# Moving columns of the matmuls read from both halves in turn

## The chip, the cores and the metric

One core of a Trainium2 chip runs the whole program. Its engines work side by side: TensorE (matmuls; PE in the profile, its weight loads PEld), VectorE (DVE), ScalarE (ACT), GpSimd (POOL) and the sync engine (SP), which here only issues transfers. TensorE writes to psum, eight banks of 512 fp32 columns on 128 partitions; DVE and ACT read it. The metric is the device time of one execution in microseconds; a kernel is told by the median of its runs.

In a matmul one operand, the weights, stands in the array, and the other, the moving one, is read column by column. A psum column comes out for each moving column.

## What is computed

```python
# x: 1 x 2048 x 576;  32 heads of 18;  F = 4608
xn = layernorm(x)                                   # no scale, no bias
q, k, v = split(xn @ wqkv)                          # per head
s = (softmax(q @ k.T * 18 ** -0.5) @ v) @ wo        # full attention
g = silu((relu(xn @ W_gate) * (xn @ W_up)) @ W_down)
return x + s * g
```

All is fp32. To keep fp32's accuracy with the faster F32R operands, the kernel splits a matrix into a high and a low part and adds three products (high·high, high·low, low·high); the probabilities and v use plain fp32 operands.

## The kernel before

**Two lanes.** Most matmuls use 64 of the 128 rows of the array, so that two of them, one on rows 0 to 63 and one on rows 64 to 127, run at once. The class `Lanes` writes out the order of the two lanes ahead of time, in Python, when the program is built. It keeps a clock for each lane, for the banks and for DVE ("V") and ACT ("A"). It counts a matmul as `cols * COL + FIX`, and each eviction by a length given in the code (0.685 for a row maximum, 0.6 for an exponential, 0.69 for the product of gate and up). It picks what each lane does next: `main` parts (sums over many matmuls) or `scores` (a matmul by itself), as banks come free. The chip then follows this order whatever the true times are; what must be waited for is waited for by semaphores.

**Stages.**
1. *Start.* Rows of x are loaded in groups of 512 tokens (`load_rows`: group 0 by four loads, groups 1 to 3 by one each). Meanwhile TensorE is warmed up (`busy`). Its 32 matmuls are 8 of ones, then groups of four: columns in order, and four forms of reading the same 512 columns (`mixed`): `b=2` (every second column first, then the others), `a=2` (0, 256, 1, 257, ...), `b=16` (steps of 16) and `a=32, c=4` (four neighbours, then a jump of 16). The last four read in order, with 32 weight columns instead of 128.
2. *Features, q, k, v.* For each group of 512 tokens, x is normalized, transposed by TensorE (`tps`) and stored as high and low parts with the tokens along the columns (`x`; spilled to `xTd`). Then come q and k (`pq`, the tokens of x moving, 512 columns; split on eviction by `split_full`, stored to `qd` and `kd`) and v (`pv`, 128 tokens of x as weights, 288 columns of `wv` moving; evicted by ACT L583, stored to `vd`).
3. *Feed-forward and attention together.* 144 units of the feed-forward net, each 128 features of F for 512 tokens: gate (`pg`) and up (`pu`), 27 matmuls of 512 columns on each, with the tokens of x moving. Two units make a cycle. `down` of an earlier pair of units runs in the same cycle: `py`, with 128 tokens of `hh` as weights and 288 columns of `dw` moving, 96 matmuls, added up in `ys`. Into this order are mixed the attention's scores: `pm` (scores of 128 queries against 512 keys, of which DVE takes the row maxima, L401) for the next pair of heads, and `psx` (128 keys against 512 queries, of which ACT takes the exponential, L891) for the present one. After a cycle, `attend` multiplies the probabilities with v in one burst (`po`, 64 records). There are eight cycles with only some maxima, then 64 with a burst each.
4. *End.* Attention output (`od`) times `wo` (`pw`, 128 rows, 288 columns moving) in groups of 128 tokens, times the gate (`gt`, from `yd` or `ys`; L1121), plus x (`xr`; L1122), stored by POOL's queue.

All matmuls but the transposes pass through `mm` (L274, L275), and so all have line 275 in the profile; the names of the tiles tell them apart. Loads pass through `load` (L271) on SP's queue, in the order of the code.

Of the kernel before, what the change touches and what calls it, by code (L numbers as in the profile page):

```python
# [9 lines left out]
F32 = mybir.dt.float32  # L10
F32R = mybir.dt.float32r
AF = mybir.ActivationFunctionType
ALU = mybir.AluOpType
# [15 lines left out]
class Lanes:  # L29


    COL, FIX, EVICT, SERVE, FENCE = 0.000446, 0.006, 0.28, 0.08, 0.15

    def __init__(self, banks, make, matmul, fence):
        self.make, self.matmul, self.fence = make, matmul, fence
# [182 lines left out]
def kernel(  # L218
# [10 lines left out]
    nc = tc.nc  # L229
    P = 128  # L230
# [13 lines left out]
    HC = D // 2  # L244
    HW = 2 * DH
# [10 lines left out]
    x2 = x.rearrange("b s d -> (b s) d")  # L256
    out2 = out.rearrange("b s d -> (b s) d")

    def rows512(t, g):
        return t[g * 512 : (g + 1) * 512, :].rearrange("(j p) d -> p j d", p=P)  # L260

    def pool(stack, name, bufs, side="left", **kw):
        return stack.enter_context(tc.tile_pool(name=name, bufs=bufs, side=side, reuse_waits="tile", **kw))
# [1 line left out]
    def keep(ins):  # L265
        return tc.keep_in_program_order(ins)
# [3 lines left out]
    def load(*args):  # L270
        ins = nc.sync.dma_start(*args)  # L271
        return keep(ins) if in_order[0] else ins

    def mm(*args, **kw):  # L274
        return keep(nc.tensor.matmul(*args, **kw))  # L275

    def tp(*args):
        return keep(nc.tensor.transpose(*args))
# [14 lines left out]
    def bank(b, name):  # L293
        return banks.tile([P, 512], F32, tag=f"b{b}", name=name)

    def fence(by, ps):
        eng = {"A": nc.scalar, "V": nc.vector}[by]
        eng.clobber_nop(outs=[eng.lower_ap(ps)])

    lanes = Lanes(8, bank, mm, fence)  # L300

    def lane_rows(lane):
        return slice(lane * R, (lane + 1) * R)

    def split_full(dhi, dlo):
        return [
            ("A", 0.6, lambda ps: nc.scalar.activation(dhi(), ps, AF.Copy)),
            ("V", 0.69, lambda ps: nc.vector.tensor_tensor(dlo(), ps, dhi().bitcast(F32), ALU.subtract)),
        ]

    def split_pool(hi, lo, raw):
# [5 lines left out]
    def pair(names, xt, ops, cols, steps):  # L317

        parts = []
        for o in range(2):  # L320
            def lane_ops(lane, o=o):
                places = [(4 * o + i, i) for i in range(KX - 1)]
                if lane == o:
                    places.append((KS - 1, KX - 1))
                rows = lane_rows(lane)
                return [
                    (lambda s=s, i=i, a=a, b=b: ops(rows, s, a, xt[o][i][rows, b, :]))
                    for s, i in places
                    for a, b in PRODUCTS
                ]  # L330

            parts.append(Part(names[o], o, [lane_ops(o), lane_ops(1 - o)], cols, steps[o]))
        return parts
# [97 lines left out]
    with ExitStack() as st:  # L431
# [19 lines left out]

        def load_rows(g):
            xt = one.tile([P, 4, D], F32, name="xt", bufs=2)
            if g == 0:
                for j in range(4):
                    load(xt[:, j], x2[j * P : (j + 1) * P, :])
            else:
                load(xt, rows512(x2, g))
            return xt

        def stats(xt, ln):
# [112 lines left out]
        def v_pairs(gw, g):  # L574
            pairs = []
            evs = {}

            def steps(j, m):
                def fn(ps):
                    if (j // 2, m) not in evs:  # L580
                        evs[j // 2, m] = [hp.tile([P, VN, 2, HW], F32, tag="hh", name="ev", bufs=4), 0]
                    ev = evs[j // 2, m]
                    nc.scalar.activation(  # L583
                        ev[0][:, :, j % 2, :], ps[:, :HC].rearrange("p (u d) -> p u d", d=HW), AF.Copy
                    )
                    ev[1] += 1
                    if ev[1] == 2:
                        t0 = g * 4 + j // 2 * 2
                        nc.gpsimd.dma_start(
                            vd[m * VN : (m + 1) * VN, :, t0 : t0 + 2, :].rearrange("u p t d -> p u (t d)"),  # L590
                            ev[0].rearrange("p u t d -> p u (t d)"),
                        )

                return [("A", 0.41, fn)]

            for j in range(4):
                js = slice(j * P, (j + 1) * P)
                pairs.append(
                    pair(
                        ("pv", "pv"), (xs[g], xs[g]),  # L600
                        lambda rows, s, a, xr, js=js: (xr[:, js], gw[rows, a, s, :]),
                        HC, [steps(j, m) for m in range(2)],
                    )
                )
            return pairs

        def busy(xt):

            ones = one.tile([P, 512], F32R, name="ones")
            xr = one.tile([P, 576], F32R, name="xr")  # L610
            root = one.tile([P, 1], F32, name="root")
            nc.gpsimd.memset(ones.bitcast(F32), 1.0)
            nc.scalar.activation(root, ident[:, :1], AF.Sqrt)
            nc.scalar.activation(xr, xt[:, 0], AF.Copy)
            ps = bank(7, "wu")
            def mixed(form, **n):
                return xr[:, :512].rearrange(f"p {form}", **n)

            ops = [(ones[:, :P], ones)] * 8 + [(xr[:, :P], xr[:, :512])] * 4
            ops += [(xr[:, :P], mixed("(a b) -> p b a", b=2))] * 4  # L620
            ops += [(xr[:, :P], mixed("(a b) -> p b a", a=2))] * 4
            ops += [(xr[:, :P], mixed("(a b) -> p b a", b=16))] * 4
            ops += [(xr[:, :P], mixed("(a b c) -> p b a c", a=32, c=4))] * 4
            ops += [(xr[:, :32], xr[:, :512])] * 4
            for l, r in ops:
                m = l.shape[1]
                to = ps[:m]
                if len(r.shape) == 3:
                    to = to.rearrange("p (a b) -> p a b", b=r.shape[2])
                if len(r.shape) == 4:  # L630
                    to = to.rearrange("p (a b c) -> p a b c", b=r.shape[2], c=r.shape[3])
                mm(to, l, r, start=True, stop=True)
            nc.scalar.activation(root, ps[:, :1], AF.Copy)

        ln0 = []
        xt0 = load_rows(0)
        busy(xt0)
        for _ in stats(xt0, ln0):
            pass
# [6 lines left out]

        qk_weights(0)
        nxt = load_rows(1)
        xn0 = one.tile([P, 4, D + DT], F32, name="xn")
        first_rows(*ln0, xn0)  # L650
# [317 lines left out]
    for k in range(0, N1, 2):  # L968
        i = k // 2
# [5 lines left out]
        n = 7 if i % 2 == 0 else 6  # L975
# [57 lines left out]
    def load_heads(k):  # L1033
        o = fo.tile([P, 5, P], F32, name="o")
        ks = slice(k * P, (k + 1) * P)
        nc.sync.dma_start(o[:, :4], od[:C4, ks].rearrange("(c p) t -> p c t", p=P))
        for d in range(2):
            nc.sync.dma_start(o[d * DT : (d + 1) * DT, 4], od[C4:, ks])
        return o

    def load_gate(k):
        if k // 4 == units[-1][0]:
            gt = ys[k % 4]
        else:
            gt = f2.tile([P, D], F32, name="gt")
            nc.sync.dma_start(gt, yd[k * P : (k + 1) * P, :])
        sg = f2.tile([P, D], F32, name="sg", bufs=2)
        nc.scalar.activation(sg, gt, AF.Sigmoid)
        nc.gpsimd.tensor_tensor(gt, gt, sg, ALU.mult)
        return gt  # L1050

    def load_res(k):
        xt = f2.tile([P, D], F32, name="xr")
        nc.sync.dma_start(xt, x2[k * P : (k + 1) * P, :])
        return xt
# [3 lines left out]
    def any_bank(name):  # L1059
        turns[0] += 1  # L1060
        return bank(turns[0] % 8, name)
# [27 lines left out]
    for j in range(4):  # L1089
        js = slice(j * P, (j + 1) * P)  # L1090
        for n in range(2):
            cs = halves[n]
            ps = any_bank("py")[:, :HC]
# [8 lines left out]
    for i, k in enumerate(horder):  # L1102
        if i + 3 < NT:
            ops_[i + 3] = load_heads(horder[i + 3])
        if i + 2 < NT:
            xts[i + 2] = load_res(horder[i + 2])
            gts[i + 2] = load_gate(horder[i + 2])
            hq[i + 2] = heads(ops_.pop(i + 2))
        hh, o5 = hq.pop(i)
        gt, xt = gts.pop(i), xts.pop(i)  # L1110
        for cs in halves:
            ps = any_bank("pw")[:, :HC]
            prs = []
            for c in range(4):
                ks = slice(c * P, (c + 1) * P)
                w = wos[c]
                prs += [(hh[:, 0, ks], w[:, 0, cs]), (hh[:, 0, ks], w[:, 1, cs]), (hh[:, 1, ks], w[:, 0, cs])]
            prs += [(o5, wos[4][:, a, cs]) for a in range(2)]
            for n, (l, w) in enumerate(prs):
                mm(ps, l, w, start=(n == 0), stop=(n == len(prs) - 1))  # L1120
            nc.vector.tensor_tensor(gt[:, cs], ps, gt[:, cs], ALU.mult)  # L1121
            nc.vector.tensor_tensor(xt[:, cs], xt[:, cs], gt[:, cs], ALU.add)  # L1122
        nc.gpsimd.dma_start(out2[k * P : (k + 1) * P, :], xt)
    acc.close()
    fin.close()
# [26 lines left out]
```

## Time and profile before

| | us |
|---|---|
| median of 3 runs | 2611.54 |
| lowest, highest | 2608.88, 2612.35 |
| profiled execution | 2609.53 |
| its span, first to last instruction | 2607.8 |
| around the span | 1.73 |

The mean granted clock of TensorE was 0.996 of full speed in the profiled execution. It read 192.79 MB from memory and wrote 44.96 MB.

How to read what follows: a group has its line, engine, operation, the tile written and those read, the shapes and the count; behind the bar its busy time, the mean ns of one, and the idle time of its engine just before it with what ended that. For matmuls, `64*128 64x512` means 64 rows and 128 weight columns, and 512 moving columns. A row of a timeline or of the chain begins with start and length in us. A matmul's record is longer than its share of the time, since the next begins before it has drained: the pace is the distance between starts.

### The profile page before, as it was taken

The numbers are of one execution on the slowest core, as the hardware profiler recorded it, in microseconds if no ns is written. First come the engines' busy times: TensorE is split into PE (matmuls) and PEld (weight loads), VectorE is DVE, ScalarE is ACT, GpSimd is POOL, SyncE is SP. The second block draws the span as 40 slices with busy tenths as digits, with TensorE's granted clock in tenths as the row PEclk, the third lists the DMA queues.
The fourth block names the chain that finished last, engine by engine and source line by source line (L and its number), as shares of the span: only waits on it lengthen the run. The fifth ranks groups of instructions, "written<-read, shape, count | busy, mean of one in ns | idle before, by whom it ended". The sixth has DMA issues, their size and how long they took to land.

```text
span 2607.8 us, 62736 instructions
## 1 busy us (share of the span) xinstructions
PE 2575.4 (99%) x25308; PEld 2106.7 (81%) x25308; DVE 1785.9 (68%) x2976; ACT 1471.0 (56%) x2763; POOL 1440.5 (55%) x1276
## 2 busy tenths in 40 slices
PE   8999999999999999999999999999999999999998
PEld 6998887777778887777778778788878777777778
DVE  4326557777777777777777777777777777776137
ACT  3221136666666666666666666666666666666662
POOL 4236885555555555555555555555555555555554
PEclk8999999999999999999999999999999999999999
DMA  7645332222332222222242222222232222222237
GB/s 240 219 150 150 88 103 69 78 70 72 98 100 66 76 69 75 69 70 75 74 133 72 71 72 67 74 66 77 72 114 82 66 77 72 74 67 58 58 113 214
DMA packets 270353, 241.85 MB, mean 93 GB/s; under 512 B 33904, under 2 KB 214896, under 8 KB 270064
## 3 DMA queue, kind: packets, MB, share of 16 engines
q1 hardware_dynamic: 262000, 209.53, 27.5%
q0 software_dynamic: 8064, 28.32, 3.3%
q8 instruction: 200, 3.28, 0.5%
q14 instruction: 89, 0.73, 0.1%
HBM read 192.79 MB, written 44.96 MB: 91 GB/s over the span
## 4 chain that ended last, share of the span: by engine, by line
PE 92%; DMA 3%; POOL 2%; DVE 1%; SPq 1%; issue 1%; ACT 0%; POOLq 0%; DVEq 0%; ACTq 0%
PE pg L275 19%; PE po L275 17%; PE py L275 16%; PE pu L275 15%; PE pm L275 10%; PE psx L275 9%; PE pq L275 3%; PE pv L275 2%; SPq L271 1%; PE pw L275 1%; DMA rgw<-in_A_wqkv_dram 0%; DMA qd<-hh 0%; DMA gt<-yd 0%; DMA rg<-in_B_W_up_dram 0%; DMA kT<-kd 0%
## 5 line engine op out<-in xcount | busy, mean ns | idle before, releaser
L401 DVE TENSOR_REDUCE mx<-pm 128x1 f32<-128x512 f32 x2048 | 1378.5, 689 | 351.5 <-PE pm L275 207.1
L891 ACT ACTIVATE p<-psx 128x512 f32<-128x512 f32 x2048 | 1181.9, 598 | 567.4 <-PE pm L275 279.3
L275 PE MATMUL pg<-x,gw 64*128 64x512 f32 x3888 | 1155.2, 391 | 1.8 <-POOL gw L313 1.8
L275 PE MATMUL pu<-x,gw 64*128 64x512 f32 x3888 | 1141.7, 391 | 0.0
L275 PE MATMUL pm<-kT,qT 54*128 54x512 f32 x2048 | 792.2, 397 | 0.7 <-DMA kT<-kd 0.7
L275 PE MATMUL psx<-qT,kT 56*128 56x512 f32 x2048 | 786.7, 394 | 0.0
L275 PEld LDWEIGHTS pg<-x,gw 64*128 64x128 f32 x3888 | 718.5, 186 | 43.4 <-POOL gw L313 2.7
L275 PEld LDWEIGHTS pu<-x,gw 64*128 64x128 f32 x3888 | 716.2, 186 | 33.5
L275 PE MATMUL py<-dw,hh 64*128 64x288 f32 x6864 | 720.3, 295 | 5.7 <-DVE ot L929 3.1
L275 PEld LDWEIGHTS py<-dw,hh 64*128 64x128 f32 x6864 | 665.4, 186 | 74.2 <-issue 53.4
L275 PE MATMUL po<-p,va 128*32 128x512 f32 x4096 | 452.7, 594 | 0.4 <-ACT p L891 0.4
L744 POOL CAST hh<-h 128x512 fp32r<-128x512 f32 x127 | 77.6, 611 | 607.2 <-DVE h L741 607.2
L313 POOL TENSOR_TENSOR gw<-rg,gw 128x1152 fp32r<-128x1152 f32 x144 | 383.7, 2665 | 11.6
L275 PEld LDWEIGHTS psx<-qT,kT 56*128 56x128 f32 x2048 | 375.3, 185 | 17.8
L275 PEld LDWEIGHTS pm<-kT,qT 54*128 54x128 f32 x2048 | 371.6, 185 | 15.6 <-DVE mx L401 0.9
L771 POOL TENSOR_TENSOR y<-yt,y 128x288 f32<-128x288 f32 x268 | 215.0, 806 | 297.8 <-ACT yt L770 297.6
L275 PEld LDWEIGHTS po<-p,va 128*32 128x32 f32 x4096 | 126.4, 110 | 279.1 <-issue 269.1
L313 POOL TENSOR_TENSOR dw<-rd,dw 128x576 fp32r<-128x576 f32 x144 | 212.2, 1474 | 11.5
L747 POOL TENSOR_TENSOR hh<-h,hh 128x512 fp32r<-128x512 f32 x144 | 186.2, 1293 | 33.2 <-ACT hh L746 23.1
L312 POOL CAST gw<-rg 128x1152 fp32r<-128x1152 f32 x144 | 165.0, 1146 | 23.4 <-DMA rg<-in_B_W_up_dram 9.5
L766 DVE TENSOR_TENSOR y<-py,y 128x288 f32<-128x288 f32 x268 | 120.0, 448 | 58.7 <-PE py L275 58.5
L929 DVE TENSOR_TENSOR ot<-po,ot 128x512 f32<-128x512 f32 x32 | 22.1, 691 | 188.4 <-PE po L275 188.4
(92 smaller groups left out, 1421.2 us busy)
## 6 DMA issues: line engine op xcount, KB each, us to landing
rd<-in_B_W_down_dram SPq DMA_DIRECT2D x144, 288.0 KB
rg<-in_B_W_gate_dram SPq DMA_DIRECT2D x144, 256.0 KB
rg<-in_B_W_up_dram SPq DMA_DIRECT2D x144, 256.0 KB
qT<-qd SPq DMA_DIRECT2D x384, 36.0 KB
kT<-kd SPq DMA_DIRECT2D x384, 36.0 KB
kd<-hh POOLq DMA_DIRECT2D x16, 512.0 KB, 5.5
qd<-hh POOLq DMA_DIRECT2D x16, 512.0 KB, 6.1
xTd<-x SPq DMA_DIRECT2D x15, 512.0 KB
```

Source lines behind the costliest of these rows:

```text
L271: ins = nc.sync.dma_start(*args)
L275: return keep(nc.tensor.matmul(*args, **kw))
L312: keep(nc.gpsimd.tensor_copy(hi, raw))
L313: keep(nc.gpsimd.tensor_tensor(lo, raw, hi.bitcast(F32), ALU.subtract))
L401: keep(nc.vector.tensor_reduce(mx[:, g % 2, h, j, c : c + 1], ps, axis=AX.X, op=ALU.max))
L744: keep(nc.gpsimd.tensor_copy(hh[:, 0], h))
L747: keep(nc.gpsimd.tensor_tensor(hh[:, 1], h, hh[:, 0].bitcast(F32), ALU.subtract))
L766: keep(nc.vector.tensor_tensor(ys[j][:, cs], ps[:, :HC], ys[j][:, cs], ALU.add))
L771: keep(nc.gpsimd.tensor_tensor(ys[j][:, cs], t, ys[j][:, cs], ALU.add))
L891: nc.scalar.activation(p[0][:, h, i, :], ps, AF.Exp, scale=SCALE)
L929: keep(nc.vector.tensor_tensor(ot, ps, ot, ALU.add))
```

## The change

`mm` reads the moving columns of every F32R matmul from the two halves in turn: with 512 columns 0, 256, 1, 257, and so on; with 288 columns 0, 144, 1, 145. The psum columns are written one after the other, so psum column 2i + o holds moving column o · n/2 + i. What reads psum, or what was loaded before, is set to this order:
- Evictions of `pq` (`split_full`) and `pv` read psum with a step of two (`apart`) and write the halves one behind the other (`both`), so q, k and v keep the order of the stored columns.
- `rows_of` loads x so that stored column j · 128 + p of a group holds token (j mod 2) · 256 + 2p + j // 2. Psum columns of matmuls with tokens moving (`pg`, `pu`, `psx`) then come out in the order of tokens, and `y` and the attention output are stored in that order as before. A group is loaded by four loads, also groups 1 to 3.
- `y` and the last product have their 288 columns in turned order alike; the last add (L1122) puts them back (`both`, `apart`).
- The warm-up is 18 matmuls of ones with 512 columns, 5 of x with 512 and 13 of x with 288, all through `mm`.
- The planner's `COL` and `FIX` are smaller: 512 columns count 0.2149 instead of 0.2344, 288 count 0.1231 instead of 0.1344.

Matmuls with fp32 operands (`po`, the transposes) read as before.

```diff
-    COL, FIX, EVICT, SERVE, FENCE = 0.000446, 0.006, 0.28, 0.08, 0.15
+    COL, FIX, EVICT, SERVE, FENCE = 0.00041, 0.005, 0.28, 0.08, 0.15
...
-    def rows512(t, g):
-        return t[g * 512 : (g + 1) * 512, :].rearrange("(j p) d -> p j d", p=P)
+    def rows_of(t, g, j):
+
+        return t[g * 512 + j % 2 * 2 * P : g * 512 + (j % 2 + 1) * 2 * P, :].rearrange("(p o) d -> p o d", o=2)[
+            :, j // 2
+        ]
...
-    def mm(*args, **kw):
-        return keep(nc.tensor.matmul(*args, **kw))
+    def mm(ps, l, r, **kw):
+
+        if r.dtype == F32R:
+            r = r.rearrange("p (o i) -> p i o", o=2)
+            ps = ps.rearrange("p (i o) -> p i o", o=2)
+        return keep(nc.tensor.matmul(ps, l, r, **kw))
+
+    def apart(ps):
+
+        return ps.rearrange("p (i o) -> p o i", o=2)
+
+    def both(t):
+        return t.rearrange("p (o i) -> p o i", o=2)
...
-            ("A", 0.6, lambda ps: nc.scalar.activation(dhi(), ps, AF.Copy)),
-            ("V", 0.69, lambda ps: nc.vector.tensor_tensor(dlo(), ps, dhi().bitcast(F32), ALU.subtract)),
+            ("A", 0.6, lambda ps: nc.scalar.activation(both(dhi()), apart(ps), AF.Copy)),
+            (
+                "V", 0.69,
+                lambda ps: nc.vector.tensor_tensor(
+                    both(dlo()), apart(ps), both(dhi().bitcast(F32)), ALU.subtract
+                ),
+            ),
...
-            if g == 0:
-                for j in range(4):
-                    load(xt[:, j], x2[j * P : (j + 1) * P, :])
-            else:
-                load(xt, rows512(x2, g))
+            for j in range(4):
+                load(xt[:, j], rows_of(x2, g, j))
...
-                        ev[0][:, :, j % 2, :], ps[:, :HC].rearrange("p (u d) -> p u d", d=HW), AF.Copy
+                        ev[0][:, :, j % 2, :].rearrange("p (o u) d -> p o u d", o=2),
+                        ps[:, :HC].rearrange("p (u d o) -> p o u d", d=HW, o=2), AF.Copy,
...
+            for i in range(36):
+                l, n = (ones, 512) if i < 18 else (xr, 512) if i < 23 else (xr, 288)
+                mm(ps[:, :n], l[:, :P], l[:, :n], start=True, stop=True)
...
-            nc.vector.tensor_tensor(xt[:, cs], xt[:, cs], gt[:, cs], ALU.add)
+            nc.vector.tensor_tensor(both(xt[:, cs]), both(xt[:, cs]), apart(gt[:, cs]), ALU.add)
```

More of the change, by code (lines that the diff above doesn't have):

```diff
@@ L615, in busy @@
             ps = bank(7, "wu")
[L616 to L632, printed above, removed]
+            for i in range(36):
+                l, n = (ones, 512) if i < 18 else (xr, 512) if i < 23 else (xr, 288)
+                mm(ps[:, :n], l[:, :P], l[:, :n], start=True, stop=True)
             nc.scalar.activation(root, ps[:, :1], AF.Copy)
```

## The prediction

> **What bounds the kernel now.** I read the page's busy times and its chain first, then the busy times by stage, then the groups of TensorE's instructions.
>
> ```profile
> PE 2575.4 (99%) x25308; PEld 2106.7 (81%) x25308; DVE 1785.9 (68%) x2976; ACT 1471.0 (56%) x2763; POOL 1440.5 (55%) x1276
> PE 92%; DMA 3%; POOL 2%; DVE 1%; SPq 1%; issue 1%; ACT 0%; POOLq 0%; DVEq 0%; ACTq 0%
> ```
>
> TensorE is busy for 99% of the span and is 92% of the chain that ends last. Busy is not peak, though, so the pace of its instructions has to be looked at. By stage (the window; then its length and each engine's busy time):
>
> ```profile
> core 0: us, PE busy (x) PEld busy (x) DVE busy (x) ACT busy (x) POOL busy (x), PEclk, DMA share, GB/s
> 0.00:61.68 61.68, 48.90 (x388) 38.18 (x389) 29.65 (x70) 20.32 (x43) 30.17 (x28) 0.92 0.74 230
> 61.68:180.53 118.85, 118.85 (x1308) 116.44 (x1310) 32.02 (x81) 34.63 (x78) 26.76 (x35) 0.98 0.54 183
> 180.53:212.00 31.47, 30.80 (x357) 30.60 (x356) 18.29 (x30) 5.51 (x12) 20.34 (x25) 1.00 0.71 226
> 212.00:404.00 192.00, 187.49 (x1918) 167.34 (x1916) 110.79 (x184) 53.24 (x105) 147.63 (x125) 1.00 0.36 102
> 404.00:2518.60 2114.60, 2114.25 (x20789) 1684.77 (x20788) 1530.56 (x2506) 1326.74 (x2468) 1169.90 (x1023) 1.00 0.26 76
> 2518.60:2607.80 89.20, 75.12 (x560) 69.36 (x560) 64.62 (x110) 30.55 (x58) 45.65 (x42) 0.95 0.72 216
> ```
>
> From 404 to 2518 us TensorE has 0.35 us without work in 2114.6. What runs there, from the groups by line and shape (count; busy time, mean ns of one), and three runs of one kind, from the chain in order of time (start, length, count):
>
> ```profile
> L275 PE MATMUL pg<-x,gw 64*128 64x512 f32 x3888 | 1155.2, 391 | 1.8 <-POOL gw L313 1.8
> L275 PE MATMUL pu<-x,gw 64*128 64x512 f32 x3888 | 1141.7, 391 | 0.0
> L275 PE MATMUL pm<-kT,qT 54*128 54x512 f32 x2048 | 792.2, 397 | 0.7 <-DMA kT<-kd 0.7
> L275 PE MATMUL psx<-qT,kT 56*128 56x512 f32 x2048 | 786.7, 394 | 0.0
> L275 PE MATMUL py<-dw,hh 64*128 64x288 f32 x6816 | 712.2, 295 | 2.7 <-POOL dw L313 1.5 <-ACTq L298 0.2
> ...
> 107.22 14.00 PE pv L275 x212
> ...
> 162.98 17.55 PE pq L275 x150
> 404.00 7.04 PE po L275 x64
> ```
>
> Two lanes of 64 rows run at once, so records count in pairs. 150 `pq` records of 512 columns are 75 pairs in 17.55 us: 0.234 us a pair. 212 `pv` of 288 columns are 106 pairs in 14.00 us: 0.132. One cycle of the main loop has 172 records of 512 columns (108 `pg` and `pu`, 32 `pm`, 32 `psx`) and 96 `py` of 288:
>
> ```profile
> 1316.10:1323.10 7.00, 7.00 (x67) 1.97 (x66) 1.07 (x3) 0.52 (x2) 6.84 (x6) 1.00 0.69 265
> 1323.10:1349.88 26.78, 26.78 (x273) 24.47 (x276) 23.68 (x37) 20.16 (x37) 11.71 (x12) 1.00 0.35 105
> ```
>
> 86 × 0.234 + 48 × 0.132 = 26.5 of the 26.78 us between two bursts of `po`. So the loop stands at the pace of its matmuls, and hardly a wait is left. `po` (7.0 us a burst, 64 bursts) has plain fp32 operands and is left as it is.
>
> **Part 1: the moving columns.** Is 0.234 us for 512 columns a floor? The warm-up at the start answers, as it runs the very form that the change gives to all: its group of four with `a=2` reads columns 0, 256, 1, 257 and so on. Counted back in fours from the last four, those with 32 weight columns (128*32), the starts are:
>
> ```profile
> 8.56 0.40 PE L275 MATMUL wu<-xr 128*128 128x512 f32 x1
> 8.79 0.38 PE L275 MATMUL wu<-xr 128*128 128x512 f32 x1
> 9.44 0.59 PE L275 MATMUL wu<-xr 128*128 128x512 f32 x1
> 11.15 0.63 PE L275 MATMUL wu<-xr 128*128 128x512 f32 x2
> 12.07 0.40 PE L275 MATMUL wu<-xr 128*32 128x512 f32 x1
> 12.77 0.39 PE L275 MATMUL wu<-xr 128*32 128x512 f32 x1
> ```
>
> - Halves in turn: 8.79 to 9.44 is three steps, 0.217 us each; rounding leaves 0.213 to 0.220. I take 0.216.
> - Columns 16 apart (`b=16`): 9.44 to 11.15, four steps of 0.43.
> - Four neighbours, then a jump (`a=32, c=4`): 11.15 to 12.07, four of 0.23.
> - In order: 12.07 to 12.77, three of 0.233. That is one lane of 128 rows, and it agrees with the two-lane 0.234: the pace belongs to reading the columns, not to there being two lanes. It comes after the faster form, so a clock still rising isn't the reason.
>
> So a pair of 512 goes from 0.234 to 0.216: 18 ns less. No row shows 2 × 144 columns. Scaled alike, 0.132 becomes 0.122: 10 ns less. Its bounds are no gain, or a loss up to the 0.43 form; I take the scaled value because it is the same form, shorter.
>
> [...]
>
> The terms:
> - `pg`, `pu`, `pm`, `psx`: 11872 records, 5936 pairs × 18 ns = 106.8 us.
> - `py`: 6816, 3408 pairs × 10 ns = 34.1 us.
> - Of these, 5 us are not had: from 212 to 404 us POOL is busy 147.63 of 192 and TensorE already idles for 4.5, so of about 13 us there I count 8.
> - `pq` and `pv` from 61.68 to 180.53, where TensorE never idles: 118.85 × 18/234, less the few transposes, 8.9 us. From 180 to 212, where loads of keys hold it in part, 1.
> - Before 61.68, nothing: the chain passes through weight loads and the stores of queries (first row below). The end likewise has output stores and gate loads on the chain; I count 2 us for its unbroken `py` and `pw`.
>
> Together 147.8 us.
>
> ```profile
> 49.66 11.03 DMA qd<-hh
> ...
> 2556.33 4.99 DMA out_dram<-xr
> ...
> 2562.27 4.38 DMA gt<-yd
> ```
>
> **Part 2: what is put back in order.** The psum columns of `pq` and `pv` are read with a step of two by ACT and DVE (36 splits, 32 copies), the residual add L1122 reads `gt` so (32 times, 288 columns). No row shows a step of two there. The nearest:
>
> ```profile
> L866 DVE TENSOR_TENSOR oT<-oT,rc 128x288 f32<-128x288 f32 x32 | 16.2, 507 | 1.1
> L1122 DVE TENSOR_TENSOR xr<-xr,y 128x288 f32<-128x288 f32 x8 | 3.7, 458 | 2.0 <-DMA xr<-in_A_x_dram 1.8
> ```
>
> L866 reads 18 of every 32 columns and takes 507 ns against 458 in order: 49 ns more. Taken for the adds: 32 × 0.05 = 1.6 us at the end, where DVE is on the chain. Bounds: nothing, or double (as TensorE's 0.43 against 0.23), 15 us. The splits and copies cost nothing either way: DVE and ACT are busy 32 and 35 us of 118.85 in that stage, and doubling them adds some 20 and 30; without that cover the banks would come free late and `pq` would wait.
>
> **Part 3: loads of x and the warm-up.** Three loads of 512 tokens become four each, nine more issues on SP, about 0.45 us apiece (four in 1.80, below). The first delays the weights queued behind it by 1.2 us, but SP then waits for a weight buffer from 9.10 to 12.96 anyway (last two rows). I take 1 us for all, 0 to 5 as bounds. The warm-up has 13 short matmuls and ends somewhat sooner; the second block of weights decides when `pq` can go on, so nothing.
>
> ```profile
> 0.74 1.80 SPq L271 DMA_DIRECT2D xt<-in_A_x_dram  x4
> ...
> 4.84 0.59 SPq L271 DMA_DIRECT2D xt<-in_A_x_dram  x1
> ...
> 8.21 0.89 SPq L271 DMA_DIRECT2D rgw<-in_A_wqkv_dram  x1
> ...
> 12.96 0.37 SPq L271
> ```
>
> The orders of tokens add no other instruction: even rows and odd rows of x go to the halves, so that columns read in turn come out in token order, and `yd`, `od` and the residual need no shuffle.
>
> **What is late next.** The stretch between bursts shrinks by 86 × 0.018 + 48 × 0.010 = 2.0 to 24.8 us; DVE's recorded 23.68 us in it become 95%. But its records overlap:
>
> ```profile
> 1324.27 0.69 DVE L401 TENSOR_REDUCE mx<-pm 128x1 f32<-128x512 f32 x1 [0.41 <-PE pm L275]
> ...
> 1349.32 1.28 DVE L401 TENSOR_REDUCE mx<-pm 128x1 f32<-128x512 f32 x2
> ```
>
> Two reductions of 0.69 in 1.28 us (second row) start 0.59 apart. 32 of them, two products and four adds are some 22 us at that pace, about 90%, and those left over fall into the burst, of whose 7.00 us DVE is busy 1.07 in the one quoted. I count 0.1 us of new waits per stretch, 64 × 0.1 = 6.4.
>
> **The sum.** 2609.5 (its span 2607.8 and 1.7 around it) − 147.8 + 6.4 + 1.6 + 1 = 2470.7. The median before is 2.0 above the profiled run's time, so 2473.
>
> **Rivals.**
> - **DVE becomes the bound.** The plan counts 32 × 0.685 + 2 × 0.69 + 4 × 0.46 = 25.1 us of DVE a cycle against 86 × 0.215 + 48 × 0.123 = 24.4 of TensorE by its new constants, and so crowds maxima to the end of a window. If DVE really needs its recorded 23.68 and gets its first maximum only 1.17 us after the burst (1324.27), nothing is spare, and irregularity costs perhaps 0.5 us a stretch: 64 × 0.4 more, 2499. Against it: the 0.59 step and the free burst. 14%.
> - **The 288 form gains nothing** (its halves are 576 bytes apart, not 1024): 34 + 3 us back, 2510. 5%.
> - **It doesn't do what it says:** two lanes are held to 0.234 by something else than the reads. Then 2611.5 + 2.6 of added work, about 2614. Against it: one lane in order has the same 0.233. 5%.
> - **Slower: four streams.** Two lanes reading two halves each keep four places open at once where the warm-up kept two. If those are too many, each column costs as in the 16-apart row: 0.43 a pair of 512, 5936 × 0.196 = 1163 us, and 3408 × 0.11 = 375 more: about 4150. It decides above 0.240 us a pair of 512, where 34 us of the `py` gain are spent. Against it: two lanes read different partitions and in order don't slow each other. 6%.
>
> **The numbers.** My forecast holds 70%. The range goes from 0.213 us a pair without new waits (about 2440) to the DVE and the 288 rivals with some waits (2525), and leaves out no more than 2 in 10. Faster by over 0.2% (what a measurement can tell): 0.70 + 0.14 + 0.05 = 0.89; within 0.2%, 0.05; slower, 0.06.
>
> **What would show it.** `pq` runs of 75 pairs in 16.2 us and `pv` of 106 in 12.9; mean records of `pg` near 374 ns instead of 391; a stretch between bursts of 24.8 to 25.0 us with DVE idle at times for TensorE. A stretch of 25.3 or more with gaps before `pm` or `po` shows DVE as the bound; L1122 near 0.5 us shows the strided add. I am wrong if `pg` stays at 391, or if the 288 pairs stay at 0.132.

## The result, and the profile after

The changed kernel takes 2525.74 us (2525.13 to 2527.83, 4 runs) against 2610.68 beside it: ratio 0.9676, interval 0.9659 to 0.9693. It is faster by 85 us, where 138 were forecast; it lies 0.7 us above the range.

The page's busy line and its chain by engine:

```profile
PE 2482.2 (98%) x25312; PEld 2056.3 (81%) x25312; DVE 1821.7 (72%) x2976; ACT 1464.6 (58%) x2763; POOL 1429.9 (57%) x1276
...
PE 90%; DMA 3%; POOL 2%; issue 2%; SPq 1%; DVE 1%; ACT 0%; POOLq 0%; DVEq 0%; ACTq 0%
```

TensorE is still busy nearly always and still the chain, so these lines look as before and don't tell where 53 us went. First the pace, from the chain in order of time and the groups by shape:

```profile
102.75 12.86 PE pv L282 x210
115.86 13.40 PE pq L282 x124
```

```profile
L282 PE MATMUL pu<-x,gw 64*128 64x512 f32 x3888 | 1085.0, 378 | 0.0
L282 PE MATMUL pg<-x,gw 64*128 64x512 f32 x3888 | 1078.3, 376 | 1.9 <-POOL gw L332 1.9
...
L282 PE MATMUL py<-dw,hh 64*128 64x288 f32 x6816 | 748.0, 289 | 5.2 <-POOL dw L332 3.7 <-ACTq L312 1.5
```

62 pairs of `pq` in 13.40 us are 0.216 us each, 105 pairs of `pv` in 12.86 are 0.1225: both as forecast, in two lanes. A record of `pg` fell from 391 to 376 ns.

Then the time, cut at the starts of the first and the last `po` burst. Before:

```profile
0.00:403.96 403.96, 386.00 (x3960) 352.53 (x3960) 190.71 (x362) 113.70 (x238) 224.87 (x213) 0.98 0.50 155
403.96:2518.64 2114.68, 2114.29 (x20790) 1684.81 (x20788) 1530.64 (x2507) 1326.78 (x2468) 1169.98 (x1023) 1.00 0.26 76
2518.64:2607.80 89.16, 75.12 (x560) 69.36 (x560) 64.58 (x110) 30.52 (x58) 45.61 (x42) 0.95 0.72 216
```

After:

```profile
0.00:383.14 383.14, 358.24 (x3964) 337.40 (x3964) 187.47 (x362) 113.48 (x238) 223.08 (x212) 0.99 0.51 163
383.14:2434.97 2051.83, 2051.83 (x20792) 1655.27 (x20790) 1568.23 (x2505) 1320.72 (x2466) 1161.35 (x1024) 1.00 0.26 78
2434.97:2524.00 89.03, 72.09 (x562) 63.62 (x561) 66.00 (x110) 30.42 (x59) 45.48 (x42) 0.96 0.70 220
```

The start gave 20.8 us, the end nothing, the loop 62.9. The forecast had about 120 for the loop. So the rest is lost there, though TensorE has a record open for all 2051.83 us. One stretch between bursts, before and after (window, length, busy times):

```profile
1255.50:1282.19 26.69, 26.69 (x268) 24.71 (x268) 23.55 (x37) 20.08 (x37) 11.59 (x12) 1.00 0.24 70
```

```profile
1211.23:1236.98 25.75, 25.75 (x272) 24.49 (x268) 22.35 (x36) 20.17 (x37) 11.45 (x11) 1.00 0.26 77
```

At the measured pace its matmuls need 86 × 0.216 + 48 × 0.1225 = 24.46 us a lane. Before, 26.69 was 0.23 above the same sum (26.46); now it is 1.29 above. The loss is steady: 59 stretches have a median of 25.74, between 25.74 and 26.02. The last four, where no maxima are left, went from 23.14–23.62 to 21.66. So something in the stretches with maxima holds a lane up about 1.05 us each: 59 × 1.05 = 62 us.

Two views name suspects. Fences (no-operations that a lane's second half of a sum waits for), by the fence's line, before and after:

```profile
L298 ACTq EVENT_SEMAPHORE  x165: 17/38/3575, 20.2 to 400.8; - x165
L298 DVEq EVENT_SEMAPHORE  x93: 21/50/6243, 24.0 to 2517.0; - x93
```

```profile
L312 ACTq EVENT_SEMAPHORE  x515: 17/38/3535, 19.1 to 2317.6; - x172
L312 DVEq EVENT_SEMAPHORE  x122: 21/50/9393, 22.5 to 2433.3; - x122
```

Before, ACT's last fence was at 400.8 us, ahead of the loop; now they go on through it. And the waits of the weight loads, after:

```profile
PEld py L282 <- DVE mx L420: 11.4, 56, 0.2
```

That is 0.2 us in nearly every stretch, for a psum bank that DVE is still reducing. Before there was one such wait (0.2 us).

### The profile page after: what moved, and what is told of

The parts are those of the page before. It is cut to its first block, busy times and chain, and to the rows that moved or that the text cites. A ratio compares the mean times of both kernels' runs of the same rounds, so it can differ in the third digit from the quotient of the medians.

```text
span 2524.0 us, 63264 instructions
## 1 busy us (share of the span) xinstructions
PE 2482.2 (98%) x25312; PEld 2056.3 (81%) x25312; DVE 1821.7 (72%) x2976; ACT 1464.6 (58%) x2763; POOL 1429.9 (57%) x1276
## 4 chain that ended last, share of the span: by engine, by line
PE 90%; DMA 3%; POOL 2%; issue 2%; SPq 1%; DVE 1%; ACT 0%; POOLq 0%; DVEq 0%; ACTq 0%
PE pg L282 19%; PE po L282 17%; PE py L282 17%; PE pu L282 13%; PE psx L282 12%; PE pm L282 8%; PE pq L282 2%; PE pv L282 2%; SPq L274 1%; DMA o<-od 1%; DMA qd<-hh 1%; DMA rgw<-in_A_wqkv_dram 1%; DMA out_dram<-xr 1%; DMA rg<-in_B_W_up_dram 0%; POOL wqk L332 0%
## 5 line engine op out<-in xcount | busy, mean ns | idle before, releaser
L420 DVE TENSOR_REDUCE mx<-pm 128x1 f32<-128x512 f32 x2048 | 1338.5, 688 | 242.0 <-PE pm L282 165.6
L282 PE MATMUL pu<-x,gw 64*128 64x512 f32 x3888 | 1085.0, 378 | 0.0
L282 PE MATMUL pg<-x,gw 64*128 64x512 f32 x3888 | 1078.3, 376 | 1.9 <-POOL gw L332 1.9
L282 PE MATMUL psx<-qT,kT 56*128 56x512 f32 x2048 | 765.5, 384 | 0.0
L282 PE MATMUL py<-dw,hh 64*128 64x288 f32 x6864 | 754.1, 289 | 5.2 <-POOL dw L332 3.7
L282 PE MATMUL pm<-kT,qT 54*128 54x512 f32 x2048 | 750.6, 380 | 0.0
L282 PEld LDWEIGHTS py<-dw,hh 64*128 64x128 f32 x6864 | 674.8, 186 | 81.5 <-issue 51.1
L332 POOL TENSOR_TENSOR dw<-rd,dw 128x576 fp32r<-128x576 f32 x144 | 203.9, 1416 | 11.5
L744 DVE TENSOR_TENSOR h<-pu,h 128x512 f32<-128x512 f32 x144 | 98.9, 687 | 79.3 <-PE py L282 47.4
```

What stands on the lines that cost most here:

```text
L282: return keep(nc.tensor.matmul(ps, l, r, **kw))
L332: keep(nc.gpsimd.tensor_tensor(lo, raw, hi.bitcast(F32), ALU.subtract))
L420: keep(nc.vector.tensor_reduce(mx[:, g % 2, h, j, c : c + 1], ps, axis=AX.X, op=ALU.max))
L744: keep(nc.vector.tensor_tensor(h, ps, h, ALU.mult))
```

## Experiments

The plan is written in Python ahead of time, so the change's new constants (`COL`, `FIX`) alter the order of the matmuls as well as the reading alters their pace. Theory A says that the loss is in the plan; theory B that DVE can't do more in any order. Further theories have their letters in the expectation in which they first stand. "Stretch" is the median of 59, from the end of one burst to the start of the next.

**The plan put back, and the plan alone.**

```diff
 # e1_old_plan: in the changed kernel
-    COL, FIX, EVICT, SERVE, FENCE = 0.00041, 0.005, 0.28, 0.08, 0.15
+    COL, FIX, EVICT, SERVE, FENCE = 0.000446, 0.006, 0.28, 0.08, 0.15
 # e2_plan_only: in the kernel before
-    COL, FIX, EVICT, SERVE, FENCE = 0.000446, 0.006, 0.28, 0.08, 0.15
+    COL, FIX, EVICT, SERVE, FENCE = 0.00041, 0.005, 0.28, 0.08, 0.15
```

> The change with the planner's COL and FIX put back to 0.000446 and 0.006, so that the order of the two lanes is planned as before and only the reading is new. Theory A (the loss is in the plan: with the smaller constants the planner believes DVE too slow, finds no free bank, and lets a lane start the second half of a sum behind a fence on ACT's or DVE's queue, 515 and 122 of them instead of 165 and 93): fences fall back to about 165 and 93, a stretch between bursts of po comes to 24.8 to 25.0 us instead of 25.74, and the time to 2470 to 2485. Theory B (DVE itself is the bound, whatever the order): the stretch stays at 25.7 and the time at 2520 to 2530.

> The kernel before, columns read in order, with only the planner's COL and FIX of the change (0.00041, 0.005). Theory A: the order that the constants give is worse by itself; ACT's fences rise to some 500 and the stretch from 26.7 to 27 to 27.7 us, the time to 2630 to 2670. Theory B: at the slow pace DVE has time for any order; the stretch stays at 26.7 and the time at 2605 to 2615.

A stretch of each:

```profile
1195.41:1220.43 25.02, 25.02 (x272) 23.33 (x268) 22.93 (x37) 19.68 (x37) 11.43 (x11) 1.00 0.26 74
```

```profile
1272.86:1300.24 27.38, 27.38 (x272) 25.67 (x274) 22.94 (x37) 20.26 (x37) 11.65 (x12) 1.00 0.24 73
```

With the old constants the changed kernel takes 2485.20 us, ratio 0.9522 (0.9508 to 0.9536), stretch 25.02: 0.2 us and 0.02 us above A's windows. The new constants alone make the kernel before slower: 2651.10, ratio 1.0156 (1.0141 to 1.0171), stretch 27.40. The fences on ACT's and DVE's queues fall to 181 and 106 in the first, and are 498 and 108 in the second. B falls: the maxima are the same, and with the old order DVE gets through them in stretches of 25.02 us instead of 25.74. And the parts add up: reading alone −126.0 us, plan alone +39.9, together −86.0; the change has −85.

**The planner's lengths.** The new constants match the new pace, so why is the plan worse? The planner counts a row maximum as 0.685 us, which is the record's length; back to back they start 0.60 apart (two of 0.69 in 1.29 us at 1235.13 in the changed kernel).

```diff
 # e3_dve_lengths
-                return qTs[u, g][rows, js], kchunk(u, c)[rows, :], [("V", 0.685, reduce)]
+                return qTs[u, g][rows, js], kchunk(u, c)[rows, :], [("V", 0.605, reduce)]
-            512, [[("A", 0.6, relu)], [("V", 0.69, times)]],
+            512, [[("A", 0.6, relu)], [("V", 0.605, times)]],
-        return [("A", 0.41, by_pool)] if side else [("V", 0.46, add)]
+        return [("A", 0.41, by_pool)] if side else [("V", 0.365, add)]
 # e4_both_lengths: these, and exp and relu 0.6 -> 0.485, copies of y 0.41 -> 0.31
 # e6_act_lengths: only those of ACT
```

> The change with three lengths of the planner set to the distance between starts that the traces show for DVE: row maximum 0.605 instead of 0.685, product of gate and up 0.605 instead of 0.69, sum of y 0.365 instead of 0.46. Theory A: the planner again finds DVE fast enough, ACT's fences fall well below 515, the stretch to 24.8 to 25.2 us and the time to 2470 to 2490. Theory B: the stretch stays at 25.7, the time at 2520 to 2530.

> As the run with DVE's lengths, and ACT's lengths too set to what the traces show (exponential and relu 0.485 instead of 0.6, copies of y 0.31 instead of 0.41). Theory A: as with DVE's lengths alone or somewhat better, 2465 to 2490. Theory B: 2520 to 2530. If ACT's lengths are what matters and DVE's don't, this one is faster than the run before it and that one isn't.

> The change with only ACT's lengths in the planner set to what the traces show (0.485 and 0.31), DVE's left at 0.685, 0.69 and 0.46. Theory A-DVE (the planner's belief about DVE alone makes the bad order): 2520 to 2530, stretch 25.7. Theory A-idle (what counts is for how long the planner finds nothing to give to a lane; its own count of that, over both lanes, is 157 us for the change, 14 with the old constants, 28 with DVE's true lengths and 52 here): 2490 to 2505, stretch 25.1 to 25.4.

| | stretch | us | ratio (interval) |
|---|---|---|---|
| the change | 25.74 | 2525.74 | 0.9676 (0.9659 to 0.9693) |
| DVE's lengths | 25.05 | 2487.81 | 0.9533 (0.9517 to 0.9549) |
| both | 25.26 | 2499.84 | 0.9576 (0.9562 to 0.9591) |
| ACT's lengths | 25.53 | 2515.95 | 0.9636 (0.9620 to 0.9652) |

With DVE's lengths alone corrected, 38 of the 40 us come back. ACT's alone give 10, between the two expectations, so neither form of A hit it; and with DVE's already right, ACT's cost 12, which no theory here said. The planner's count of time in which it had nothing for a lane (its steps of 0.02 us counted while the program is built: 157 us for the change, 14 with the old constants, 28 and 29 with DVE's and both lengths, 52 with ACT's) follows the trend only roughly: both lengths have 29 and a stretch of 25.26, the dearer fences below have 45 and a stretch of 25.05.

**Are the fences the cost?**

```diff
 # e7_no_fence
-            elif self.main[lane] and self.fenced(lane, self.main[lane][0]):
+            elif not (waiting(0) + waiting(1)) and self.main[lane] and self.fenced(lane, self.main[lane][0]):
 # e8_dve_fence: DVE's lengths as above, and
-    COL, FIX, EVICT, SERVE, FENCE = 0.00041, 0.005, 0.28, 0.08, 0.15
+    COL, FIX, EVICT, SERVE, FENCE = 0.00041, 0.005, 0.28, 0.08, 0.6
```

> The change with the planner forbidden to fence a second half as long as scores are left to place; it waits instead until a bank or a synchronized sum is there. Theory F (the fences on ACT's and DVE's queues are what costs): with few of them left in the loop the stretch falls to 25.0 to 25.3 and the time to 2480 to 2500. Theory A-idle (the planner's idle time, here 176 us over both lanes against 157, is what costs, with fences or without): 2520 to 2540, stretch 25.7 to 26.0.

> The change with DVE's true lengths and with a fence counted as 0.6 us instead of 0.15, so that the second half of a sum is planned later behind it. Theory A-idle (planner's own idle 45 us against 28 with DVE's lengths alone): 2490 to 2500, somewhat slower than that run's 2487.8. Theory F: faster than it, 2470 to 2485, since lanes then find the fence passed.

Forbidden so, the fences on ACT's queue end at 366.8 us:

```profile
L312 ACTq EVENT_SEMAPHORE  x165: 17/38/3195, 18.6 to 366.8; - x165
L312 DVEq EVENT_SEMAPHORE  x101: 21/50/5735, 22.1 to 2443.3; - x101
```

The stretch stays at 25.74 us, and the time is 2535.56 (0.9711, 0.9696 to 0.9725); the 10 us more are lost ahead of the loop, where the first burst starts 10 us later than in the changed kernel. Dearer fences: 25.05 and 2491.33 (0.9540, 0.9526 to 0.9555). So theory F falls. The 515 fences were the most striking difference of the two traces, and they are no measure of the loss: with DVE's lengths corrected there are 644 on both queues against 637, in a stretch of 25.05.

```profile
L312 ACTq EVENT_SEMAPHORE  x406: 17/38/3717, 19.4 to 2277.7; - x136
L312 DVEq EVENT_SEMAPHORE  x238: 21/50/9424, 22.8 to 2394.0; - x119
```

**Is it the readers of the banks?** The same order, with less to do for DVE (row maxima over half the columns) or ACT (exponentials over half; `po` then reads these 256 columns twice, which is not printed here).

```diff
 # e12_half_max; e13_half_max_old_plan has the old COL and FIX too
-                    keep(nc.vector.tensor_reduce(mx[:, g % 2, h, j, c : c + 1], ps, axis=AX.X, op=ALU.max))
+                    keep(nc.vector.tensor_reduce(mx[:, g % 2, h, j, c : c + 1], ps[:, :256], axis=AX.X, op=ALU.max))
-                    nc.scalar.activation(p[0][:, h, i, :], ps, AF.Exp, scale=SCALE)
+                    nc.scalar.activation(p[0][:, h, i, :], ps, AF.Exp, scale=SCALE / 16)
 # e14_half_exp; e15_half_both: this and e12's
-                    nc.scalar.activation(p[0][:, h, i, :], ps, AF.Exp, scale=SCALE)
+                    nc.scalar.activation(p[0][:, h, i, :256], ps[:, :256], AF.Exp, scale=SCALE / 16)
```

> The change, its plan untouched, with DVE's row maxima taken over 256 of the 512 columns (half the keys are left out of the maxima, and the scale in the exponential is a sixteenth so that it stays finite). Same order, same fences; a psum bank of pm comes free about 0.25 us sooner. Theory D (at the places where the planner had nothing to give, the next sum takes a bank that DVE is still reading, and TensorE really waits for it): the stretch falls from 25.74 to 24.8 to 25.2 us and the time to 2470 to 2495. Theory O (the order holds the lanes up by itself, by their turns and by ACT's queue, and DVE is no part of it): 25.6 to 25.75, 2515 to 2530.

> The change with the planner's old COL and FIX and with DVE's row maxima over 256 of the 512 columns (half the keys left out, scale a sixteenth). What is left of DVE in that order's stretch of 25.02: theory D says little, 24.7 to 25.0, 2465 to 2485; if DVE's speed were the bound of every order, 24.5 or less, 2455 or less.

> The change, its plan untouched, with ACT's exponentials over 256 of the 512 columns (the other queries are left out, the scale is a sixteenth, and po reads the 256 twice, so a burst of po may have another length: only the stretch between bursts counts). A bank of psx comes free about 0.2 us sooner. Theory K (the plan, believing DVE's banks still taken, hands the few others out again at once, and TensorE waits for the way from a psx through ACT's exponential back to its bank): the stretch falls from 25.74 to 25.3 or less. Theory O (turns of the lanes and halves of sums that follow one another hold TensorE up, and no reader's speed matters): 25.6 to 25.75.

> As the run before with DVE's row maxima over 256 columns too. Theory K: 24.8 to 25.1, the wait is for readers of banks, DVE's or ACT's, whichever the order has put last. Theory O: still 25.5 or more.

A stretch with half the maxima, and one with both halved:

```profile
1210.02:1235.63 25.61, 25.61 (x272) 24.28 (x268) 15.91 (x37) 20.07 (x37) 11.44 (x12) 1.00 0.26 78
```

```profile
1203.56:1228.89 25.33, 25.33 (x272) 24.03 (x276) 16.01 (x38) 13.85 (x38) 11.31 (x12) 1.00 0.28 79
```

DVE's busy time falls from 22.35 to 15.91 and the stretch by 0.14 us only (2520.61 us, 0.9649, 0.9633 to 0.9665): theory D falls, and O's windows hold both. Half the exponentials give 0.03 (25.72, as O has it; one run, 2536.09). Both together 0.41 (25.33; one run, 2508.84), neither K's 24.8 to 25.1 nor O's 25.5. With the old plan, halving the maxima leaves 24.99 of 25.02 (2483.20; 0.9506, 0.9492 to 0.9520): there DVE holds nothing up.

The trace tells where the lanes are held. By the starts of the matmuls (the two lanes told apart by their pace), both lanes together fall 2.2 us behind their pace in a stretch of the changed kernel, 1.6 of it at three places, some 17, 22 and 24.5 us in; with the old constants it is 0.8 in all. At these places weight loads start as soon as a reader has given its bank back. The first place, in the stretch that starts at 1211.23:

```profile
1227.88 0.60 ACT L894 ACTIVATE p<-psx 128x512 f32<-128x512 f32 x1
...
1228.45 0.18 PEld L282 LDWEIGHTS py<-dw,hh 64*128 64x128 f32 x1 [0.21 <-DVE mx L420]
1228.53 0.18 PEld L282 LDWEIGHTS psx<-qT,kT 56*128 56x128 f32 x1
```

The load for `py` waited for DVE. The load for `psx` starts 0.05 us after ACT's exponential has ended (1228.48), and the list of waits doesn't count it, since the other lane's load leaves no idle time before it. With half the maxima the 56 waits of `py` for DVE are gone from the list, and the stretch is only 0.14 us shorter; with both halved the list still has two loads of `pm` released by copies of y (L773, 0.6 us in all), which no run shortened. What follows: the order makes the lanes wait for readers of banks at a few places, and a quicker DVE alone (0.14 us) or a quicker ACT alone (0.03) leaves most of the wait. Of the lost microsecond some 0.4 goes when both are quicker; how the rest is shared between the order itself and the readers that no run shortened is not settled.

**A mixed plan.** New constants for the start, old ones for the loop (one line, `lanes.COL, lanes.FIX = 0.000446, 0.006`, ahead of the first cycle).

> The change with its own COL and FIX up to the feed-forward's first cycle and the old ones from there on. The start from the changed plan (first burst 2.8 us sooner than with the old constants) and the loop from the old one: 2482 to 2486, the fastest so far if the two add up; 2486 to 2490 if the first burst's gain is lost again.

2485.91 us (0.9523, 0.9510 to 0.9536), the same as the old constants throughout (the intervals overlap). It lies in the window of the two gains added up, but the first burst came 1.0 us sooner and not 2.8. The old constants in the changed kernel beat both kernels and are the simplest.

**How many places can be read in turn?**

```diff
 # e5_forms: the warm-up; form() rearranges xr[:, :n]
-            for i in range(36):
+            forms = [xr[:, :512]] * 6
+            forms += [form("(o i) -> p i o", o=2)] * 6
+            forms += [form("(o i) -> p i o", o=4)] * 6
+            forms += [form("(o i) -> p i o", o=8)] * 6
+            forms += [form("(o i c) -> p i o c", o=2, c=2)] * 6
+            forms += [form("(o i c) -> p i o c", o=2, c=4)] * 6
+            forms += [xr[:, :288]] * 6
+            forms += [form("(o i) -> p i o", n=288, o=2)] * 6
+            forms += [form("(o i) -> p i o", n=288, o=4)] * 6
```

> The change with a longer warm-up that reads the same columns in several forms, six matmuls each on all 128 rows, after 24 of ones: 512 in order, in turn from 2, 4 and 8 parts, from two halves by twos and by fours, then 288 in order and in turn from 2 and 4 parts. [...] Theory S (a small number of places can be open at once; two is the most): 4 and 8 parts fall to 0.3 to 0.43.

The first start of each group of six, and of the group behind them (timeline: start, length):

```profile
9.31 0.39 PE L656 MATMUL wu<-xr 128*128 128x512 f32 x1
10.67 0.38 PE L656 MATMUL wu<-xr 128*128 128x512 f32 x1
11.97 0.44 PE L656 MATMUL wu<-xr 128*128 128x512 f32 x1
13.65 0.68 PE L656 MATMUL wu<-xr 128*128 128x512 f32 x1
16.57 0.53 PE L656 MATMUL wu<-xr 128*128 128x512 f32 x1
18.56 0.42 PE L656 MATMUL wu<-xr 128*128 128x512 f32 x1
20.08 0.43 PE L656 MATMUL wu<-xr 128*128 128x288 f32 x2
20.88 0.41 PE L656 MATMUL wu<-xr 128*128 128x288 f32 x2
21.61 0.47 PE L656 MATMUL wu<-xr 128*128 128x288 f32 x2
22.53 0.31 PE L656 MATMUL wu<-xr 128*128 128x64 f32 x2
```

The distance of two starts, by six, is the pace: in order 0.227, two parts 0.217, four 0.280, eight 0.487, two parts by twos 0.332, by fours 0.253. For 288 columns: 0.133 in order, 0.122 in two parts, 0.153 in four. S is right only in that two parts gain while four lose 0.05 us and eight more: its window was 0.3 to 0.43, and by its count of places alone the two forms with neighbours, which also read from two, should not be slower than in order. The number of places and the distance between them change together here, so the reason for the pace stays open. (One run, 2538.30 us, with a longer warm-up: the first burst came at 393.8 us.)

## Why the prediction was wrong

Step by step, as the prediction put them:

- **Part 1, the pace: right.** 0.216 and 0.1225 measured, 0.216 and 0.122 taken. Scaling the 288 form from the 512 one held.
- **The terms: nearly right in the start, by luck in the end.** For the start 8.9 + 1 + 8 less 1 for SP were taken, and 20.8 came; 2.8 of them belong to the plan, since with the old constants the first burst starts at 385.9 us instead of 383.1. For the end a gain of 2 and a cost of 1.6 were taken, and 0.13 came: the cost did not come, as the next point shows, and so the gain did not either.
- **Part 2, the strided add: too dear.** Its record takes 460 ns as a rule where it took 457 (least, median, longest of 24, before and after):

```profile
L1122 DVE TENSOR_TENSOR xr<-xr,gt x24: 444/457/1696, 2541.4 to 2593.0; 128x288 f32<-128x288 f32 x24
L1125 DVE TENSOR_TENSOR xr<-xr,gt x24: 445/460/2991, 2457.9 to 2510.0; 128x288 f32<-128x288 f32 x24
```

  So the step of two costs this add 3 ns in the median. The mean rose from 554 to 829 ns because 8 of the 24 last over 1.1 us, where 2 did before; with the new constants alone, and no step, there are 5 such, so they don't come from the step. What holds them is open; the stage took no longer (89.03 us against 89.16).
- **What is late next: the step that failed.** It counted 0.1 us of new waits per stretch, 6.4 us in all. Measured: 1.05 us in each of 59, 62 us. I took DVE's true pace (0.59 between starts) for the question of what comes late, and the order of the work isn't made with that pace: the planner uses 0.685. By its count DVE needs 25.1 us a cycle, and against 26.6 of TensorE by the old constants there was room for that; the new ones left 24.4. I put 25.1 and 24.4 in a rival, as a crowding with a price of 0.5, instead of pricing the plan as a part of the change. Run by itself the new plan costs 0.70 a stretch (26.70 to 27.40) and 39.9 us. The rest, 0.33, comes with the faster pace in the old order as well (25.02 stands 0.56 above its matmuls, before it was 0.23): that too was sized at 0.1. That the plan costs this is shown; that it does so through its count of DVE's time fits the run with DVE's lengths (25.05), but doesn't explain why ACT's true lengths then cost 12 us.
- **The rivals.** "DVE becomes the bound" named the plan's crowding, which was right, but made DVE's own speed the condition, which was not: DVE halved gives 0.14 us. Its price of 0.5 a stretch was half of what came. The 288 rival and "two lanes are held by something else" fell with the pace. "Four streams" fell for two lanes, which read other partitions (0.216 a pair); in one lane four places do cost (0.280).

## What to carry to other kernels

A plan made ahead of time from constants is part of the program: when one engine's pace changes, the lengths it counts for the others decide the order, and a pessimistic one that was harmless can cost a third of the gain (40 of 126 us here). Run the new pace with the old order, and the new order at the old pace, before reading the sum of both; here the two added up to within 1 us. And a trace's most striking difference (350 more fences) need not be the cost: take it away by itself first.

## What was not expected of the hardware

- Reading moving fp32r columns from two halves in turn takes 0.216 us for 512 where reading in order takes 0.227 to 0.234; but four parts take 0.280, eight 0.487, and pairs of neighbours from two halves 0.332. Why is open.
- Two lanes with two places each keep 0.216, where one lane with four places takes 0.280, so what costs in one lane isn't the number of places of both together.
- DVE adds with a step of two over 288 columns as fast as in order (medians of 460 and 457 ns).
